# A hand-ordered RWKV and Hyena kernel with a new order of operations, banks, engine choices and POOL waits

## The chip, the cores and the metric

The kernel runs on one NeuronCore of a Trainium2 chip. The core has five engines, each with its own instruction queue that it works off strictly in order: PE (TensorE, matrix products, written to the eight banks of PSUM), DVE (VectorE), ACT (ScalarE), POOL (GpSimd) and SP (SyncE, which here only issues DMA transfers). The engines wait for one another through semaphores. The metric is the time of one execution on the device in microseconds (us).

## The reference

Two layers follow each other, in float32, for 4 batches of 768 steps with 8 heads of 48 (384 channels):

```python
for t in range(S):                                   # RWKV
    cur = np.einsum('bhd,bhe->bhde', u[None] * kt, vt)
    y[:, :, t] = np.einsum('bhd,bhde->bhe', rt, state + cur)
    state = wt[:, :, :, None] * state + np.einsum('bhd,bhe->bhde', kt, vt)
...
proj = x @ w_proj                                    # Hyena gate, x = y with heads side by side
x1, x2, x3 = proj[..., :D], proj[..., D:2*D], proj[..., 2*D:]
x2_conv = np.fft.irfft(np.fft.rfft(x2, axis=1) * np.fft.rfft(filter_fft, axis=0), n=S, axis=1)
return (x1 * x2_conv * x3) @ w_out
```

## The kernel before, in words

The 768 steps of a batch are cut into 6 chunks of 128, 24 chunks in all. `group` (line 1286) makes the operations that two neighbouring chunks share (the first two chunks go alone, so there are 13 groups: 0 is chunk 0, 1 is chunk 1, 2 is chunks 2 and 3, up to 12 for chunks 22 and 23). `first` (line 1321) makes those of one chunk. `early` (line 1495) and `spectrum` make the Fourier matrices and the spectrum of the filter, `second` (line 1593) the Hyena layer of one batch.

An operation has a name, and the string `ORDER` (line 45) has one line for each: the name, a letter for the engine, the PSUM bank if it opens one, and at the end, for POOL operations, the name of a DVE operation for which it is to wait although it needs nothing of it (a "tie"; the tie keeps POOL away from the SBUF port that it shares with DVE). `Plan.run` (line 1069) issues the operations in the order of this string, which is then each engine's program order; nothing else is scheduled. Letters: P, Q and F are PE (three ways of one product), A and N ACT, D, V and M DVE, G and C POOL, S SP, and a dash says that the operation is left out because its neighbour does its work. `warm n b` issues n/2 matmuls of 512 columns into bank b that nobody reads ("fillers", line 1225).

The names that matter below, i a chunk, g a group, b a batch:

- loads, on SP: `lw`, `lk`, `lr`, `lv` with i (192 KB each), `u`, three `lwproj`, `lwout`, `filt`
- head: `ur` and `um`, `ub` spread u over the partitions (copy, matmul, copy); `ang`, `sin`, `maps`, `masks`, `ia`, `is` make masks and Fourier matrices; `table` loads ACT's function table; `if` (line 1531) and `in` (line 1539) write signed copies of the inverse Fourier matrix, `in` with two products with -1.0, of 768 and of 192 elements a partition; `kz` clears padding
- RWKV: `ln`g logarithm of w, `cs`i its running sums on PE, `ex`i their exponentials, `kq`i products with k and r, `tr`i and `qk`i transposes and their copy, `sc`i scores, `mt`i masked scores (`mc`i is the mask when POOL makes it), `kv`i, `ki`i and `su`i the state, `rk`g = r times k, `ru`g times u, `rh`g adds the halves, `cc`g sums them, `vb`g is v in bf16, `vc`g is `vb` times `cc`; `yi`i, `ys`i, `y`i collect the output on PE, `xn`i copies it (with V it also adds `vc`, and `yi` is left out), `yt`i and `xT`i transpose it
- Hyena: `p`, `q` (with b, columns, half) and `xw` are the three projections, `cp`, `cq`, `cxw` their copies or products, `gq` the gate product if `cq` was only a copy, `sd`b.z.n sums and differences of the two halves of x2, `f` the forward transform, `cf` its copy, `u0`b, `u1`b and `p`b the product with the filter's spectrum (two products, one sum), `E` the inverse transform, `cE`, `aE`, `dE`, `yE` its copy, sums and gating, `o`, `co`, `so` the output product, its copy and its store; `h`, `hg`, `hc`, `fsd` are the filter's spectrum

An operation on two chunks works on tiles of 128 partitions by 768 elements. The buffers are few (line 41): three for w, four for k and r, four for v, and 8 PSUM banks for all products, so an order also sets when buffers come free.

Of the kernel before, what the change touches and what calls it, by code (L numbers as in the profile page):

```python
# [44 lines left out]
ORDER = """  # L45
table sin
wz D
pads D
lw3 S
u S  # L50
kz2 G
lw1 S
lw0 S
lk1 S
maps G
kz3 G
smalls D
lr0 S
lw2 S
lr1 S  # L60
lk0 S
ang2 D
lk2 S
lr2 S
lk3 S
lv0 S
ur A
warm 7 6
um P 7
ub A  # L70
sin2 A
ang1 D
sin1 A
kz1 G ang1
ang0 D
sin0 A
table exp
ln1 A
masks G ang0
imaps G ang0  # L80
ln0 A
lr3 S
lw5 S
lr4 S
lv1 S
lw4 S
ia2 G ang0
lv3 S
lv2 S
lk4 S  # L90
warm 32 5
cs1 P 6
lr5 S
lk5 S
cs0 P 1
ex1 A
kz0 D
kq1 D
warm 12 5
tr1 P 0  # L100
ex0 A
lwproj0 S
rk1 G
kq0 D
# [24 lines left out]
vb0 A
mt1.0 M  # L130
warm 7 2
tr2 P 5
lwproj1 S
qk2 A
lr7 S
mt1.1 -
sc0 P 2
sc2 P 4
mt2.0 M
mc2.0 -  # L140
mt2.1 -
mt0.1 -
mc0.1 -
mc1.1 -
lr6 S
lk7 S
lk6 S
table sin
is A
lv7 S  # L150
lw8 S
lv6 S
filt S
lw9 S
lr9 S
lk8 S
lk9 S
lr8 S
vb1 A
lv9 S  # L160
lv8 S
rh0 G
kv0 P 0
su0 D
mt0.0 M
mc0.0 -
warm 21 1
ki1 P 2
kv1 P
cc0 D  # L170
table exp
ln3 A
kq3 D
mc1.0 -
mc2.1 -
vb2 A
rk2 G
ph3 A
cc1 D
ru2 D  # L180
rh2 D
warm 4 5
tr3 P 3
# [12 lines left out]
kq4 D
vc2 G rh2
kv2 P
yi0 P 6
ph4 A  # L200
yt1 P 3
cs5 P 4
xT1 A
ex5 A
yi2 - 0
lw11 S
lw10 S
# [12 lines left out]
yt0 P 7  # L220
lk10 S
lr11 S
lr10 S
lwout S
rk3 G rh2
lk11 S
ru3 D
ki3 P 2
tr5 P 3
yt2 P 6  # L230
rh3 D
# [12 lines left out]
cc3 D
ys3 P
mt4.0 M
vb3 A
sc5 P 2
mt5.0 N
ln4 A  # L250
lw13 S
lw12 S
mt5.1 -
mc4.1 -
mt3.1 -
mc3.1 -
p0.0.0 P 0
y3 P
xn3 V
mc4.0 -  # L260
mc5.1 -
vc3 G rh3
lr12 S
lk13 S
lk12 S
cp0.0.0 A
ki4 P 4
kv4 P
# [12 lines left out]
yt3 P 2
xT4 A
y5 P
cp0.2.0 A
xT3 A
q0.0.0 P 6
xn5 V
if G
cq0.0.0 D
yt5 P 2  # L290
cs7 P 4
cs6 P 0
cwproj1 A
ex7 A
xw0.0 P 6
cxw0.0 A
xT5 D
xw0.2 P 2
xw0.4 P 6
kq7 D  # L300
rk4 G
ex6 A
ph7 A
cxw0.2 A
# [12 lines left out]
sd0.0.0 D
cc4 D
q0.0.1 P 4
sd0.1.0 D  # L320
sc7 P 2
qk6 A
sc6 P 0
mt6.1 -
cq0.0.1 D
mt6.0 M
mc6.0 -
gq0.0.1 -
vb4 A
f0.0 P 6  # L330
kv6 P 4
q0.2.1 P 5
mt7.0 N
su6 D
cq0.2.1 D
vc4 G sd0.1.0
cf0.0 A
mt7.1 -
mc7.1 -
mc6.1 -  # L340
mc7.0 C sd0.1.0
in A
yi6 P 2
y6 P
xn6 A
yi7 P 0
f0.2 P 6
ki7 P 4
ys7 P
kv7 P  # L350
ln5 A
lw15 S
# [48 lines left out]
u00.0 D
u10.0 D
p0.0 D
lw16 S
# [3 lines left out]
ru5 G fsd1  # L408
rh5 G
cxw1.0 A  # L410
sc9 P 4
q0.2.0 P 7
cc5 D
cq0.2.0 D
su9 D
gq0.2.1 -
lw17 S
lk16 S
mt8.1 -
# [12 lines left out]
kq11 D
cwout A
E0.0 P 4
E0.1 P 6
mc8.0 C p0.0
ph10 A
vc5 G p0.0
cE0.1 A
lr16 S  # L440
ph11 A
yi8 P 0
ys8 P
cE0.0 A
mc9.1 -
gq0.0.0 -
aE0.1.0 D
aE0.1.1 D
aE0.0.0 D
aE0.0.1 D  # L450
dE0.0.1 -
dE0.1.1 -
mc8.1 -
y8 P
E0.2 P 2
vb6 A
tr10 P 6
xn8 A
tr11 P 0
cE0.2 A  # L460
qk10 A
ki10 P 5
yt8 P 4
kv10 P
qk11 A
aE0.2.1 D
aE0.2.0 D
sc10 P 6
xT8 A
sc11 P 0  # L470
# [453 lines left out]
sd3.0.1 D
sd3.1.2 D
E2.1 Q 6
cq3.0.0 D
sd3.1.1 G sd3.1.2
co1.0 A
co1.1 A  # L930
# [8 lines left out]
aE2.1.1 D
aE2.1.0 D  # L940
sd3.0.0 G gq2.0.1
p3.2.0 P 0
# [3 lines left out]
aE2.2.1 D
aE2.2.0 D
cp3.2.0 A
dE2.2.0 D
# [96 lines left out]
"""

class Op:  # L1050
# [824 lines left out]
```

## Time and profile before

| what | us |
|---|---|
| runs | 156.36 (median), 155.32 and 156.45 |
| the profiled execution, its own time | 155.63 |
| its span, first to last instruction | 153.5 |

The profile's page names engines as above; PEld is PE's load of weights, which runs beside its products. Busy shares are over the span, and the lines with an L are lines of the kernel's file. In views in order of time each row begins with the start and the length in us, and a bracket at its end gives the idle time of the engine ahead of it and what ended it. In rows of groups, `x11 | 20.0, 1819 | 15.8` means 11 instructions, 20.0 us in all, 1819 ns for one, and 15.8 us of idle time just ahead of them. The most costly groups are spread thin: none of them is over 28 of the 153.5 us. DMA moves 27.40 MB in 104117 packets, of which 100129 are under 512 bytes.

### The profile page before, as it was taken

To read this page: it belongs to the slowest core of one execution; us is meant where nothing else is said; L and a number is where in the kernel's file an instruction comes from. 1 tells how busy PE (TensorE), PEld (TensorE's weight loads), DVE (VectorE), ACT (ScalarE), POOL (GpSimd) and SP (SyncE) were. 2 spreads that over 40 slices of the span, in tenths; PEclk is the share of its full clock that TensorE was granted. 3 is DMA by queue.
4 is the path that set the end of the run, shared out by engine and by line. 5 is a ranking of instruction groups with operands and counts; after the bars stand their busy time and mean duration, and the time that the engine had idled before them with its cause. 6 is when DMAs were issued, how large, how long until landed. Compare 5 with 4: busy or idle time off the path is not lost.

```text
span 153.5 us, 4271 instructions
## 1 busy us (share of the span) xinstructions
PE 141.5 (92%) x1666; PEld 89.0 (58%) x1666; DVE 127.9 (83%) x237; ACT 128.0 (83%) x225; POOL 76.9 (50%) x85
## 2 busy tenths in 40 slices
PE   4999888799999998999999999999999999999880
PEld 1345446556657564677666676686767665655530
DVE  6307894976599999999999699999999899999930
ACT  4868998897999999895999898998999557774570
POOL 7822949189541563997072913469461801410310
PEclk9999999999999999999999999999999999999999
DMA  4999979899899899999898999989940000700185
GB/s 86 218 207 221 218 150 268 157 345 204 184 315 208 155 192 279 195 212 211 159 207 163 225 193 207 216 168 204 275 161 4 0 4 0 307 0 4 70 323 223
DMA packets 104117, 27.40 MB, mean 178 GB/s; under 512 B 100129, under 2 KB 102690, under 8 KB 104098
## 3 DMA queue, kind: packets, MB, share of 16 engines
q1 hardware_dynamic: 104098, 27.14, 77.8%
q8 instruction: 13, 0.21, 0.6%
q14 instruction: 6, 0.05, 0.1%
HBM read 22.41 MB, written 4.72 MB: 177 GB/s over the span
## 4 chain that ended last, share of the span: by engine, by line
PE 53%; DVE 27%; ACT 8%; issue 4%; POOL 2%; DMA 1%; POOLq 1%; ACTq 0%; SPq 0%; DVEq 0%
PE banks L1600 11%; PE banks L1640 6%; DVE U L1189 6%; PE banks L1350 5%; PE banks L1490 4%; PE banks L1225 4%; PE banks L1362 4%; PE banks L1441 3%; PE banks L1776 3%; DVE kq L1338 3%; ACT banks L1335 3%; DVE mt L1378 2%; PE banks L1704 2%; PE banks L1461 2%; DVE P L1677 2%
## 5 line engine op out<-in xcount | busy, mean ns | idle before, releaser
L1189 POOL TENSOR_TENSOR rk<-kr 128x768 bf16<-128x768 f32 (+1 forms) x13 | 22.0, 1693 | 21.6 <-DMA kr<-in_r_dram 6.9
L1338 DVE TENSOR_TENSOR kq<-banks,kr 128x768 bf16<-128x768 f32 x24 | 22.5, 952 | 10.3 <-ACT banks L1335 10.2
L1600 PE MATMUL banks<-xT,wproj 128*128 128x384 bf16 x144 | 27.5, 326 | 0.0
L1189 POOL TENSOR_TENSOR vc<-vb,cc 128x768 bf16<-128x768 bf16 (+1 forms) x13 | 17.8, 1375 | 16.6 <-ACT vb L1193 6.8
L1193 ACT ACTIVATE x<-banks 128x768 bf16<-128x768 f32 (+1 forms) x29 | 20.1, 704 | 3.1 <-PE banks L1640 1.5
L1335 ACT ACTIVATE banks<-banks 128x768 f32<-128x768 f32 x24 | 19.0, 809 | 1.9 <-PE banks L1332 1.3
L1378 DVE TENSOR_TENSOR mt<-banks,mask_excl 128x1024 bf16<-128x1024 f32 (+1 forms) x17 | 18.9, 1124 | 0.8 <-PE banks L1362 0.7
L1600 PEld LDWEIGHTS <-wproj 128*128 128x128 bf16 x144 | 12.8, 97 | 7.3 <-issue 0.3
L1234 ACT ACTIVATE qk<-banks 128x512 f32<-128x512 f32 x24 | 14.0, 599 | 1.4 <-PE banks L1350 1.2
L1350 PE MATMUL banks<-ident,kq 128*128 128x128 bf16 x192 | 13.9, 219 | 0.8 <-ACT X L1193 0.3
L1225 PE MATMUL banks<-wt 128*128 128x512 bf16 (+1 forms) x43 | 13.3, 464 | 1.1 <-DVE wt L1256 1.1
L1776 PE MATMUL banks<-wout,y 128*128 128x384 bf16 x72 | 13.5, 326 | 0.6 <-DVE g L1626 0.5
L1490 PE MATMUL banks<-sd,F 128*128 128x384 bf16 (+1 forms) x96 | 13.7, 327 | 0.0
L1640 PE MATMUL banks<-wproj,xT 128*128 128x384 bf16 x72 | 13.4, 326 | 0.1
L1350 PEld LDWEIGHTS <-kq 128*128 128x128 bf16 x192 | 11.4, 97 | 3.4 <-DVE kq L1338 2.0
L1193 ACT ACTIVATE o<-banks 128x768 f32<-128x768 f32 (+1 forms) x13 | 9.6, 762 | 3.5 <-PE banks L1776 3.5
L1453 DVE TENSOR_TENSOR xn<-banks,vc 128x384 bf16<-128x384 f32 x17 | 9.2, 551 | 3.5 <-PE banks L1441 3.5
L1383 POOL TENSOR_SCALAR_AFFINE_SELECT mt<-mt 128x1024 bf16<-128x1024 bf16 (+1 forms) x10 | 9.5, 954 | 5.0 <-ACT banks L1335 4.0
L1193 ACT ACTIVATE X<-banks 128x768 bf16<-128x768 f32 x12 | 9.7, 809 | 2.8 <-PE banks L1490 2.8
L1189 DVE TENSOR_TENSOR U<-X,hh 128x2304 bf16<-128x2304 bf16 (+1 forms) x12 | 11.5, 995 | 0.0
L1490 PEld LDWEIGHTS <-F 128*128 128x128 bf16 (+1 forms) x120 | 8.3, 104 | 5.3 <-issue 0.9
L1704 PE MATMUL banks<-mi,P 128*128 128x384 bf16 (+1 forms) x62 | 10.4, 300 | 0.6 <-ACT banks L1335 0.6
(109 smaller groups left out, 309.1 us busy)
## 6 DMA issues: line engine op xcount, KB each, us to landing
w<-in_w_dram SPq DMA_DIRECT2D x24, 192.0 KB, 3.7
kr<-in_k_dram SPq DMA_DIRECT2D x24, 192.0 KB, 4.0
kr<-in_r_dram SPq DMA_DIRECT2D x24, 192.0 KB, 3.9
v<-in_v_dram SPq DMA_DIRECT2D x24, 192.0 KB, 4.1
out_dram<-o SPq DMA_DIRECT2D x11, 384.0 KB, 2.7
y<-in_moe_w_proj_dram SPq DMA_DIRECT2D x2, 576.0 KB, 5.5
U<-in_moe_filter_fft_dram SPq DMA_DIRECT2D x1, 1152.0 KB, 6.7
sd<-in_moe_w_proj_dram SPq DMA_DIRECT2D x1, 576.0 KB, 5.8
```

The costliest lines, as they stand in the source:

```text
L1189: return eng(e).tensor_mul(o, a, b)
L1193: return nc.scalar.activation(out=o, in_=a, func=AF.Copy)
L1225: nc.tensor.matmul(banks[:, int(at), 0:256 * z], wt[:, 0:L], _mid(wt, z), start=True, stop=True)
L1234: nc.scalar.activation(out=o.bitcast(FP32), in_=a.bitcast(FP32), func=AF.Copy)
L1335: op(f"ex{i}", [ACT], lambda e, bk: nc.scalar.activation(out=two(bk, f"cs{i}")[:, :, 0:C], in_=two(bk, f"cs{i}")[:, :, 0:C], func=AF.Exp), ...
L1338: op(f"kq{i}", [DVE], lambda e, bk: nc.vector.tensor_mul(kq[f][:, :, :, 0:D], two(bk, f"cs{i}")[:, :, 0:C].rearrange("p a (h d) -> p a h d ...
L1350: nc.tensor.transpose(p[:, HP * m + j, :], kq[f][:, m, 2 * j:2 * j + 2, :], ident)
L1378: return copy(ACT, o, x) if e in (ACT, ACT2) else nc.vector.tensor_mul(o, x, _mid(mask_excl, z - HP * a))
L1490: nc.tensor.matmul(p[rows], F[:, ti, c0 + rows.start:c0 + rows.stop], x[q][:, ti, :], start=(ti == 0), stop=(ti == NT - 1),)
L1600: nc.tensor.matmul(p, wproj[:, cb, col0:col0 + L], xT[bx][:, NT * hf:NT * hf + NT, cb, :], start=(cb == 0), stop=(cb == CB - 1),)
L1640: nc.tensor.matmul(view(bk)[:, z], xT[bx][:, c0 + z, cb, :], wproj[:, cb, C:2 * C], start=(cb == 0), stop=(cb == CB - 1),)
L1776: nc.tensor.matmul(view(bk)[:, z], yt_[:, z, :], wout[:, cb, :], start=(cb == 0), stop=(cb == CB - 1),)
```

## The change

Only the string `ORDER` is changed; no function is. The operations are the same 990, with the same dependences; what changes is the order on each engine's queue, the bank of 41 of them, the engine of 51, POOL's ties, and the fillers.

- Head: `u` and `ur` come first; `table sin` goes behind `ur`; the 32 fillers go ahead of everything else on PE, `um` behind `cs2`; the loads of r2 and v0 go ahead of k1, w2 and r1. `kz1` to `kz3`, `ia0`, `ia2`, `rk0`, `rh0`, `rh1`, `qk2` and the masked scores of chunks 0 and 2 go to DVE; `kz0`, `ia1` and `rh2` to POOL. Fillers grow from 83 to 101 (each counts for 256 columns).
- Before 45 us: `ru3`, `rh3` and `vb3` go to POOL (from DVE, DVE and ACT), `in` goes from ACT to POOL, where it stands behind `if` and ahead of `rk4`; `vc2` from POOL to DVE; `cp0.0.0`, `xT3`, `xT4` and `cxw0.2` from ACT to DVE. `sd0.0.0` stands ahead of `ru4` on DVE. `yi0` on PE is left out, `xn0` on DVE adds what it added.
- Middle: `rh5` to DVE; `rh7`, `ru9`, `rh10`, `rh11` and `ru12` to POOL; `xT12`, `xT16`, `xT18` and `xT20` from ACT to DVE; `cq0.2.1` and `cq2.2.1` to ACT as copies, for which `gq0.2.1` and `gq2.2.1` come up on DVE.
- Tail: `gq2.0.0` goes ahead of `xn23`, `dE1.2.0` behind it; `sd3.1.2` and `gq3.2.1` to POOL, `cq3.2.1` to ACT, `gq3.2.0` and `co3.2` to DVE; `yE3.1.0` on POOL loses its tie to `yE3.0.0`.
- Ties: most of POOL's ties name an earlier DVE operation than before, some are gone.

```diff
--- before.py
+++ after.py
@@ -42,1006 +42,1009 @@
...
-ORDER = """
+ORDER = """u S
+ur A
...
+kz2 D
...
+warm 32 5
...
+table exp
...
-kz2 G
...
-ur A
...
+cs1 P 0
...
-um P 7
...
+um P 6
...
+warm 2 7
...
+warm 12 1
...
+warm 2 3
...
+table sin
...
+warm 21 5
...
-warm 32 5
-cs1 P 6
...
-warm 12 5
...
-warm 7 2
...
-table sin
...
+warm 7 7
...
+warm 4 2
...
+vc2 D
...
+rk3 G cc0
...
+warm 2 3
...
+yi0 - 6
...
-warm 21 1
...
-table exp
...
-warm 4 5
...
-vc2 G rh2
...
-yi0 P 6
...
+ru3 G cc2
...
+rh3 G
...
-rk3 G rh2
...
-ru3 D
...
-rh3 D
...
+vb3 G xn2
...
+warm 12 4
...
-vb3 A
...
+if G su4
...
+in G
...
-if G
...
+rk4 G xn5
...
-rk4 G
...
+sd0.0.0 D
...
-sd0.0.0 D
...
+vc4 G kq6
...
-cq0.2.1 D
-vc4 G sd0.1.0
...
-in A
...
+cq0.2.1 A
...
+gq0.2.1 D
...
 kq9 D
...
+ru5 G su7
...
+rh5 D
...
+u00.0 D
...
-u00.0 D
...
-p0.0 D
...
-ru5 G fsd1
-rh5 G
...
+p0.0 D
+mc8.0 C u00.0
...
-gq0.2.1 -
...
-mc8.0 C p0.0
...
-yE0.1 D
...
-rk8 G yE0.2
...
+yE0.1 D
...
+rk8 G kq15
...
+u11.0 D
...
+ru10 G u11.0
...
+rh10 G cq1.2.1
...
-u11.0 D
...
-ru10 G p1.0
...
-rh10 D
...
+rh11 G aE1.0.1
...
-rh11 D
...
-ru12 D
...
+ru12 G
...
+dE1.2.1 D
...
+vc12 G yE1.0
...
-vc12 G yE1.0
...
-dE1.2.1 D
...
-gq2.2.1 -
+gq2.0.0 D
...
-dE1.2.0 D
...
-dE1.1.1 G dE1.2.0
...
+dE1.1.1 G mt23.0
...
+dE1.2.0 D
...
-gq2.0.0 D
...
+gq2.2.1 D
...
+sd3.0.2 D
...
 sd3.0.1 D
-sd3.1.2 D
...
+sd3.1.2 G sd3.0.2
...
-sd3.0.2 D
...
+cq3.2.1 A
...
-cq3.2.1 D
...
-gq3.2.1 -
...
+gq3.2.0 D
...
+gq3.2.1 G gq3.2.0
...
-gq3.2.0 G gq3.0.1
...
-yE3.1.0 G yE3.0.0
...
+yE3.1.0 G
...
-co3.2 A
...
+co3.2 D
...
```

More of the change, by code (lines that the diff above doesn't have):

```diff
@@ L134 @@
[L134 to L147, printed above, removed]
-table sin
-is A
-lv7 S
+ln1 A
+lr4 S
+lw5 S
+masks G ang0
+ln2 A
+imaps G kz3
+ia2 D
+lr3 S
+lv3 S
+cs1 P 0
+warm 7 6
+cs2 P 4
+ex1 A
+kq1 D
+um P 6
+vb0 A
+ln0 A
+ph1 A
+lv2 S
+lw4 S
+ub A
+warm 2 7
+tr1 P 0
+lv1 S
+ex2 A
+cs0 P 2
+rk1 G ang1
+ia0 D
+lr5 S
+lv5 S
+lk4 S
+ex0 A
+lk5 S
+kq2 D
+kq0 D
+warm 12 1
+qk1 A
+cs3 P 6
+ph0 A
+rk0 D
+ru1 D
+sc1 P 0
+lv4 S
+mt1.0 M
+mt1.1 -
+lwproj0 S
@@ L151 @@
+lw7 S
+lwproj2 S
+lw6 S
+ia1 G
+ex3 A
+ph2 A
+warm 2 3
+kv0 P 5
+lwproj1 S
+table sin
+lr6 S
+tr0 P 4
+tr2 P 3
+lk7 S
+su0 D
+warm 21 5
+lr7 S
+qk2 D
+kq3 D
+sc2 P 0
+qk0 A
+is A
+sc0 P 2
+lk6 S
+table exp
+ph3 A
+ru0 G
+mt2.1 A
+ln3 A
+vb1 A
+rk2 G mt1.0
+rh1 D
+rh0 D
+ru2 D
+cc1 D
+tr3 P 5
+warm 7 7
+mt0.1 D
+mt0.0 D
 lw8 S
 lv6 S
+mc1.0 -
+lv7 S
+mt2.0 D
+cc0 D
+vb2 A
+mc2.0 -
+warm 4 2
 filt S
 lw9 S
+qk3 A
+lk9 S
 lr9 S
+cs4 P 0
+ki1 P 2
+rh2 G ru2
+mc0.0 -
+mc2.1 G ru2
+ex4 A
+cc2 D
+vc2 D
@@ L243 @@
+kv3 P
+rh3 G
+yt0 P 3
+mc3.0 -
+mt3.1 -
+mc3.1 -
+cwproj0 A
 su3 D
 cc3 D
-ys3 P
+qk5 A
+qk4 A
+xT0 A
+lw11 S
+yi3 - 0
+yt2 P 6
+lr11 S
+ys3 P
+vb3 G xn2
+y3 P
+warm 12 4
+sc5 P 2
+sc4 P 4
+lk10 S
+xn3 V
+lwout S
+xT2 A
+lr10 S
 mt4.0 M
-vb3 A
-sc5 P 2
 mt5.0 N
-ln4 A
-lw13 S
-lw12 S
+mt4.1 -
+ki4 P 7
+yt3 P 6
+p0.0.0 P 0
+vc3 G mt3.0
 mt5.1 -
+cp0.0.0 D
+p0.2.0 P 5
 mc4.1 -
[L255 to L259, printed above, removed]
-mc4.0 -
[L261 to L268, printed above, removed]
@@ L439 @@
-cE0.1 A
-lr16 S
-ph11 A
 yi8 P 0
 ys8 P
+kq11 D
+gq0.0.0 -
+mc8.1 -
+lv14 S
+gq0.2.0 -
+cE0.1 A
+ph11 A
+rk6 G rh5
+y8 P
 cE0.0 A
-mc9.1 -
-gq0.0.0 -
 aE0.1.0 D
-aE0.1.1 D
[L449 to L458, printed above, removed]
+xn8 A
+aE0.0.1 D
+vb6 A
+E0.2 P 2
+tr10 P 1
+aE0.0.0 D
+aE0.1.1 D
+cE0.2 A
 tr11 P 0
-cE0.2 A
 qk10 A
+yt8 P 4
+qk11 A
+aE0.2.0 D
+lv15 S
+ru6 G aE0.0.0
+aE0.2.1 D
 ki10 P 5
-yt8 P 4
 kv10 P
-qk11 A
-aE0.2.1 D
-aE0.2.0 D
+lk17 S
 sc10 P 6
+su10 D
@@ L820 @@
 f2.1 P 0
-rh11 D
+sc20 P 6
+so0.0 S
 cc11 D
-vc11 G rh11
-sc20 P 6
 ph22 A
@@ L926 @@
[L926 to L930, printed above, removed]
+o1.2 P 0
 cE2.1 A
-o1.2 P 0
+E2.2 Q 2
+aE2.1.1 D
 co1.2 A
-E2.2 Q 2
+sd3.1.1 G p2.0
 cE2.2 A
-gq2.0.1 D
 E2.0 Q 4
+aE2.1.0 D
 cE2.0 A
[L939 to L942, printed above, removed]
+p3.2.0 P 1
+gq3.0.0 -
+aE2.2.0 D
+aE2.2.1 D
+sd3.1.2 G sd3.0.2
+dE2.1.0 D
+so1.0 S
 f3.2 P 6
+cp3.2.0 A
 f3.2.1 P
-sd3.0.2 D
[L946 to L949, printed above, removed]
 aE2.0.1 D
-dE2.2.1 G dE2.2.0
+aE2.0.0 D
 cf3.2 A
-aE2.0.0 D
+sd3.0.0 G
 dE2.0.0 D
-u03.2 D
```

1087 lines of the change are left out of this document (502 added, 585 removed).

## The prediction, made before the changed kernel was run

> **What bounds the kernel now.** I read the page's first part, then the engines' busy time in five stretches, then the chain of work that ended last, and then single stretches in order of time.
>
> ```profile
> span 153.5 us, 4271 instructions
> ...
> PE 141.5 (92%) x1666; PEld 89.0 (58%) x1666; DVE 127.9 (83%) x237; ACT 128.0 (83%) x225; POOL 76.9 (50%) x85
> ```
>
> The shares say little, because the limit changes. The stretches (start and end, length, busy time of PE, PEld, DVE, ACT and POOL, granted clock, DMA share, GB/s) show it:
>
> ```profile
> 0.00:10.20 10.20, 8.12 (x22) 2.73 (x23) 4.05 (x27) 6.99 (x9) 6.88 (x27) 1.00 0.84 167
> 10.20:36.90 26.70, 23.39 (x337) 14.92 (x335) 19.68 (x33) 23.98 (x42) 16.94 (x18) 1.00 1.01 223
> 36.90:67.40 30.50, 29.10 (x350) 18.36 (x351) 27.41 (x42) 29.26 (x52) 17.50 (x14) 1.00 1.00 218
> 67.40:122.60 55.20, 55.04 (x791) 38.05 (x790) 52.35 (x88) 49.34 (x93) 30.45 (x24) 1.00 0.82 173
> 122.60:153.50 30.90, 25.86 (x172) 14.97 (x169) 24.41 (x50) 18.43 (x32) 5.16 (x6) 0.99 0.30 116
> ```
>
> From 10 to 67 us the DMA engines are full (1.01 and 1.00). From 67 to 123 PE is busy 55.04 of 55.20 us: nothing but less matmul work shortens that. In the last stretch DVE is busy 24.41 us. So a gain can come from the head, from what DVE loses between about 40 and 60, or from the tail. The chain (start, length, what) says the same of both ends; the last line is DVE's own last run, to 147.39:
>
> ```profile
> 4.22 6.13 PE banks L1225 x16
> 10.79 0.80 ACT banks L1335
> ...
> 144.84 0.37 DVE y L1189
> ...
> 145.34 0.95 POOLq L1870
> ...
> 146.33 1.98 PE banks L1776 x11
> ...
> 146.22 1.17 DVE L1189 TENSOR_TENSOR y<-y,g 128x384 bf16<-128x384 bf16 x4
> ```
>
> It begins with 16 filler matmuls (line 1225) and, near the end, passes through one POOL product.
>
> **The change, part by part.** The sum is made against the profiled execution, 155.63 us, which lies 0.73 below the median of 156.36.
>
> *Head.* Now the fillers stand behind um, which waits for u, and cs1 stands behind the fillers:
>
> ```profile
> 8.53 0.94 ACT L1301 ACTIVATE lg<-w 128x384 bf16<-128x384 f32 x2
> 10.79 1.50 ACT L1335 ACTIVATE banks<-banks 128x768 f32<-128x768 f32 x2 [1.32 <-PE banks L1332]
> ...
> 37.66 0.96 DVE L1338 TENSOR_TENSOR kq<-banks,kr 128x768 bf16<-128x768 f32 x1 [0.54 <-ACT banks L1335]
> 39.65 0.96 DVE L1338 TENSOR_TENSOR kq<-banks,kr 128x768 bf16<-128x768 f32 x1 [1.03 <-ACT banks L1335]
> ...
> 31.05 4.17 SPq L1295 DMA_DIRECT2D kr<-in_k_dram x2
> ...
> DMA to landing us min/median/max: 3.6/6.3/6.7
> ```
>
> After the change the fillers come first and u's copy stands ahead of the sine table's load, so ln1 stays near 8.5 to 9.0, while cs1 no longer waits for fillers. ex1 then starts behind ln1 and ln2, near 9.9 instead of 10.79: 0.9 us early. In SP's queue u goes ahead of w3, and r2 and v0 ahead of k1: the load of r1, for kq1, is the eighth large one where it was the seventh, 192 KB at 167 GB/s or 1.2 us later, which can eat the lead at once. And it is not kept in any case. kq6 (39.65) needs the k load of chunk 6, the second of the pair that is issued from 31.05 to 35.2; with the shortest landing of 3.6 us after its issue it cannot be there before 38.8, and the queue ahead of it holds the same loads in both orders. So at most 0.85 us of lead survives at 40, and I keep 0.25. If the DMA cover were gone, the whole 0.9 would stay. Eighteen more fillers of 256 columns are queued (101 for 83); by the chain's 6.13 / 32 = 0.19 us each they cost at most 3.4 us, on a PE that idles 26.70 - 23.39 = 3.3 us in that stretch, and below nothing they cannot go. I take zero, since each stands where the next matmul waits for a copy, and leave their harm to the upper end.
>
> *POOL from rk3 to rk4.* ru3, rh3 and vb3 move to POOL, into one idle time; `in`, the two negations of line 1542, moves from ACT into another:
>
> ```profile
> 31.22 1.48 POOL L1189 TENSOR_TENSOR vc<-vb,cc 128x768 bf16<-128x768 bf16 x1 [3.62 <-ACT vb L1193]
> ...
> 39.51 1.82 POOL L1189 TENSOR_TENSOR rk<-kr 128x768 bf16<-128x768 f32 x1 [0.97 <-issue]
> ...
> L1189 POOL TENSOR_TENSOR rk<-rk,u_b 128x768 bf16<-128x768 bf16 x3 | 4.9, 1639 | 3.0 <-DVE P L1677 2.9
> L1311 POOL TENSOR_TENSOR rk<-rk 128x384 bf16<-128x384 bf16 x2 | 1.8, 910 | 0.2
> L1195 POOL CAST vb<-v 128x768 bf16<-128x768 f32 x1 | 0.8, 822 | 2.7 <-DVE sd L1651 2.7
> L1536 POOL TENSOR_SCALAR mi<-mi 128x384 bf16<-128x384 bf16 x1 | 1.2, 1167 | 0.0
> ...
> 41.36 0.56 DVE L1189 TENSOR_TENSOR rk<-rk,u_b 128x768 bf16<-128x768 bf16 x1 [0.75 <-POOL rk L1189]
> ```
>
> The three cost 1.64 + 0.91 + 0.82 = 3.37 us and fit into 3.62. `in` writes 768 + 192 = 960 elements a partition. No row shows it on POOL. Low end, at the cast's 822/768 ns an element: 1.0 us. High end, at L1536's 1167/384: 2.9 us. L1536 is the nearest, also a product with -1.0 on the same tile, so I take 2.9. Of it 0.97 is idle time; vc2's move to DVE lets rk3 and all behind it start earlier by up to a product's 1.48; I take 0.6, an estimate, since rk3 waits for loads too. rk4 so comes 2.9 - 0.97 - 0.6 = 1.3 later, and ru4 on DVE starts as rk4 ends, as it does now at 41.36. Against that, the new order puts sd0.0.0 (0.75) ahead of ru4, into the wait. Net 0.3 to 0.7 us later on DVE at 45; I take 0.5 (with the low end it would be 0.6 early). Behind rk4 on POOL stands vc4, and y6 on PE waits for vc4 through yi6; PE has room there, as f0.0 and q0.2.1 stand in between. The Trainium skill, page "GPSIMD Engine Reference", section "Engine selection", calls one-input operations on GpSimd roughly line-rate; by that `in` would cost about the low end and the sum would be 1.1 us better; the L1536 row differs.
>
> *DVE from 45 to 63.* cq0.2.1 leaves DVE (0.55); its later product gq0.2.1 and rh5 come to it (0.355 each): +0.16. Two losses go. kq9 waits 0.37 for its exponential, which stood behind `in` on ACT. And U's first product meets POOL's rh5:
>
> ```profile
> 50.01 0.96 DVE L1338 TENSOR_TENSOR kq<-banks,kr 128x768 bf16<-128x768 f32 x1 [0.37 <-ACT banks L1335]
> ...
> L1189 DVE TENSOR_TENSOR U<-X,hh x2: 1343/1610/1876, 55.5 to 57.3; 128x2304 bf16<-128x2304 bf16 x2
> ...
> 55.26 0.91 POOL L1311 TENSOR_TENSOR rk<-rk 128x384 bf16<-128x384 bf16 x1
> ...
> L1626 DVE TENSOR_TENSOR g<-banks,x 128x384 bf16<-128x384 f32 x7 | 3.9, 550 | 0.0
> L1311 DVE TENSOR_TENSOR rk<-rk 128x384 bf16<-128x384 bf16 x9 | 3.2, 355 | 0.2
> L1189 DVE TENSOR_TENSOR y<-y,g 128x384 bf16<-128x384 bf16 x5 | 1.5, 355 | 0.1
> ```
>
> The same product took 1.876 and 1.343 us: the first, from 55.50, ended 1.2 us after rh5 did, so it stood until POOL was done. With rh5 on DVE 0.53 us are saved. Together 0.16 - 0.37 - 0.53 = -0.74, and with +0.5 from above -0.25 at 63. If the loads held DVE back again, this would be zero.
>
> *From 63 to 123.* The same matmuls run (yi0, two of them, goes), on a full PE; some 16 operations change engine or waits. New waits of DVE are those of cc10, cc11, cc12 and rh9 on halves and products that POOL now makes (0.91 and 1.64, above); behind each waits DVE's whole queue, but other work stands between, and POOL is busy only 30.45 of these 55.20 us. I take 0, with -0.5 to +1.0 for small waits.
>
> *Tail.* After xn23, DVE loses gq2.0.0 (now ahead of it), sd3.1.2 (to POOL) and cq3.2.1 (to ACT), and gains dE1.2.0, gq2.2.1 and gq3.2.0:
>
> ```profile
> L1189 DVE TENSOR_TENSOR g<-g,x 128x768 bf16<-128x768 bf16 x3 | 1.8, 598 | 0.0
> L1651 DVE TENSOR_TENSOR sd<-x 128x384 bf16<-128x384 bf16 x4 | 1.3, 368 | 0.0
> L1747 DVE TENSOR_TENSOR y<-y 128x384 bf16<-128x384 bf16 x7 | 2.4, 358 | 0.1
> ...
> 130.47 0.69 DVE L1189 TENSOR_TENSOR g<-g,x 128x768 bf16<-128x768 bf16 x1
> ...
> 145.36 0.91 POOL L1189 TENSOR_TENSOR y<-y,g 128x384 bf16<-128x384 bf16 x1 [1.43 <-DVE y L1189]
> ```
>
> That is 0.60 + 0.37 + 0.55 = 1.52 out and 0.36 + 0.355 + 0.355 = 1.07 in: -0.45. The stretched gq2.0.1 (0.69) may lose 0.1. yE3.1.0 on POOL no longer waits for yE3.0.0: it ends near 145.3 instead of 146.27. Next late is the last product of block 2, inside DVE's run of four from 146.22, so only some 0.25 of that 1.0 reaches the end. co3.2 on DVE beside co3.3 on ACT gives at most 0.1, since its store follows co3.3's on SP. Tail: -0.8, from -0.3 to -1.2.
>
> Sum: -0.25 - 0.8 = -1.05. The profiled execution would be 154.6, the median 156.36 - 1.05 = 155.3.
>
> **Rivals.**
>
> *More.* `in` at its low end (-1.1) and the head's 0.65 kept: 155.3 - 1.75 = 153.6. For it: ACT is relieved of several copies where it was busy 23.98 of 26.70. Against it: the DMA share of 1.01.
>
> *Nothing moves.* The loads hold everything up to 67, and in the tail another wait takes POOL's place: 155.3 + 0.25 + 0.5 = 156.05. For it: DMA and PE are full in turn, for 112 of 153 us.
>
> *Slower: POOL takes the port first.* Many POOL operations are now tied to the operation before a DVE product with two SBUF tiles, not to that product: mc8.0 ahead of p0.0, ru10 ahead of p1.0, rk8 ahead of yE0.1, vc12 ahead of dE1.2.1, dE1.1.1 ahead of gq2.0.0, sd3.1.2 ahead of sd3.0.1. All is well if DVE asks first.
>
> ```profile
> 97.69 1.35 DVE L1189 TENSOR_TENSOR U<-X,hh 128x2304 bf16<-128x2304 bf16 x1
> 99.08 1.36 DVE L1677 TENSOR_TENSOR P<-U 128x2304 bf16<-128x2304 bf16 x1
> ...
> 100.58 1.64 POOL L1189 TENSOR_TENSOR rk<-rk,u_b 128x768 bf16<-128x768 bf16 x1 [2.89 <-DVE P L1677]
> ```
>
> DVE's next product began 0.04 us after the one that it needs (97.69 + 1.35 = 99.04, then 99.08); a released POOL operation began 0.14 after (99.08 + 1.36 = 100.44, then 100.58). The margin is 0.1 us, for DVE. Where it fails, DVE loses the POOL operation's length, 0.9 to 1.8 us; it decides as soon as one longer than the gain of 1.05 is lost. One at 1.3 gives 156.6, three give 155.3 + 3.9 = 159.2. The Trainium skill, page "Perfetto Trace Analysis", section "Optimizing Scalar/DVE Operations", warns that moving work between DVE and GpSimd might not help, because they share a port; here ru10's 1.64 us lie beside unstretched DVE work.
>
> **How the numbers follow.** About 1% (1.56 us, so 154.8 and 157.9) is what a measurement of this kernel can tell from no change. Forecast, 154.3 to 156.0: 0.47. More, 153.0 to 154.3: 0.22. Nothing, 156.0 to 156.6: 0.17. Slower, above 156.6: 0.14. Faster by over 1% is the second case and a quarter of the first, 0.34; slower by over 1% is most of the last, 0.12; the rest is 0.54. The range leaves out the lower half of the second case and two thirds of the last, 0.2: 153.6 to 157.2.
>
> **What would show it.** Right: cs1 near 9.0; the two POOL negations of `in` at about 2.9 us together, rk4 near 41; U's products both 1.35; PE still full from 67 to 123; POOL's yE3.1.0 ending before DVE's yE3.0.0 does. Wrong: any DVE product with two SBUF inputs stretched by more than 0.5 us, PE gaps between 67 and 123 adding to over 1 us, or kq6 starting before 38.8.

## The result and the profile after

| | before | after |
|---|---|---|
| median of 20 runs each, us | 156.22 (155.16 to 158.38) | 157.06 (156.28 to 158.05) |
| the profiled execution, its own time, us | 155.63 | 156.87 |
| its span, us | 153.5 | 155.2 |

The ratio of after to before is 1.0062, with a 95% interval from 1.0038 to 1.0087. The changed kernel is 0.6 to 1.4 us slower, where 1.05 us less was forecast. Every ratio here and below leaves out runs more than 1.5% above the fastest of their kernel and is taken against runs of the kernel before made beside them on the same chip; medians are of all runs. First the head of the page after, then its five stretches (start and end, length, busy time of PE, PEld, DVE, ACT and POOL, granted clock, DMA share, GB/s):

```profile
span 155.2 us, 4297 instructions
...
PE 142.7 (92%) x1673; PEld 90.5 (58%) x1673; DVE 132.4 (85%) x250; ACT 125.4 (81%) x216; POOL 90.3 (58%) x88
```

```profile
0.00:10.20 10.20, 8.38 (x33) 3.45 (x33) 4.36 (x31) 9.34 (x12) 4.45 (x22) 1.00 0.81 162
10.20:36.90 26.70, 23.61 (x328) 14.92 (x328) 22.24 (x39) 20.52 (x36) 19.22 (x18) 1.00 1.03 232
36.90:67.40 30.50, 27.47 (x292) 16.89 (x291) 27.06 (x40) 25.14 (x44) 19.11 (x13) 0.94 0.95 208
67.40:122.60 55.20, 55.19 (x806) 38.49 (x804) 52.23 (x87) 50.70 (x95) 39.16 (x29) 1.00 0.82 168
122.60:155.20 32.60, 28.04 (x222) 16.73 (x220) 26.53 (x55) 19.69 (x33) 8.32 (x9) 0.98 0.31 122
```

The third row is the odd one. Before, PE issued 350 matmuls there; now it issues 292, and the granted clock is 0.94 where it was 1.00. To see where the time went, the rows of both timelines were matched operation by operation, by their order on each engine:

| operation | before | after | later by |
|---|---|---|---|
| kq6 ends (DVE) | 40.61 | 41.10 | 0.49 |
| rk4 ends (POOL) | 41.33 | 44.27 | 2.95 |
| cq0.0.1 ends (DVE) | 44.97 | 47.38 | 2.41 |
| h1 starts (PE) | 49.44 | 53.15 | 3.71 |
| p0.0 ends (DVE) | 60.04 | 63.26 | 3.22 |
| yi8 starts (PE) | 62.76 | 65.70 | 2.94 |
| y23 starts (PE) | 122.26 | 124.63 | 2.37 |
| co3.2 ends (last copy) | 149.91 | 151.38 | 1.47 |

So 3.7 us are lost between 38 and 53 us, and 2.2 of them come back later. The loss starts on POOL. This is POOL's timeline of the changed kernel (start, length, in brackets the idle time ahead and what ended it):

```profile
39.17 3.32 POOL L1547 TENSOR_SCALAR mn<-mi 128x768 bf16<-128x768 bf16 x2
42.46 1.82 POOL L1192 TENSOR_TENSOR rk<-kr 128x768 bf16<-128x768 f32 x1
...
49.54 2.24 POOL L1192 TENSOR_TENSOR rk<-kr 128x768 bf16<-128x768 f32 x1 [0.65 <-DMA kr<-in_k_dram]
```

The first row is `in`, the second rk4 behind it, the third rk5, which a load releases. DVE's timeline shows both effects:

```profile
41.18 0.76 DVE L1654 TENSOR_TENSOR sd<-x 128x1152 bf16<-128x1152 bf16 x1
44.31 0.56 DVE L1192 TENSOR_TENSOR rk<-rk,u_b 128x768 bf16<-128x768 bf16 x1 [2.37 <-POOL rk L1192]
...
46.43 0.95 DVE L1629 TENSOR_TENSOR g<-banks,x 128x768 bf16<-128x768 f32 x1
...
48.70 4.29 DVE L1556 TENSOR_TENSOR P<-U 128x1152 bf16<-128x1152 f32 x2
```

DVE idles 2.37 us for rk4 (0.75 before). The last row is fsd0 and fsd1 with 4.29 us for the two, where the same two took 46.75 to 49.37, 2.62, before: fsd1 alone took 2.96 instead of 1.35, because it overlaps rk5 from 49.54 to 51.77. The row `g<-banks,x` is cq0.0.1, which empties PSUM bank 4. Before, the kernel had these rows for cq0.0.1, fsd0 with fsd1, kv6 and f0.2:

```profile
44.02 0.95 DVE L1626 TENSOR_TENSOR g<-banks,x 128x768 bf16<-128x768 f32 x1
...
46.75 2.62 DVE L1553 TENSOR_TENSOR P<-U 128x1152 bf16<-128x1152 f32 x2
...
45.03 0.31 PE L1403 MATMUL banks<-vb,kq 128*64 128x48 bf16 x8
...
46.54 1.14 PE L1490 MATMUL banks<-sd,F 128*128 128x384 bf16 x6
```

On PE of the changed kernel, kv6 needs bank 4:

```profile
44.20 1.15 PE L1493 MATMUL banks<-sd,F 128*128 128x384 bf16 x6
47.44 0.31 PE L1406 MATMUL banks<-vb,kq 128*64 128x48 bf16 x8 [2.09 <-DVE g L1629]
...
48.95 2.09 PE L1493 MATMUL banks<-sd,F 128*128 128x384 bf16 x6
```

PE idles 2.09 us ahead of kv6. Behind the gap, the six matmuls of f0.2, of the same form as those in the first row (f0.0), take 2.09 us instead of 1.15. The same stretch in windows of 1 us shows the clock:

```profile
45.00:46.00 1.00, 0.35 (x3) 0.00 (x0) 0.96 (x3) 0.80 (x2) 0.00 (x0) 1.00 0.88 171
46.00:47.00 1.00, 0.00 (x0) 0.00 (x0) 1.00 (x2) 0.20 (x1) 0.65 (x1) 1.00 1.15 231
47.00:48.00 1.00, 0.56 (x10) 0.41 (x11) 1.00 (x2) 0.00 (x0) 1.00 (x2) 1.00 1.03 204
48.00:49.00 1.00, 1.00 (x14) 0.68 (x12) 1.00 (x3) 0.48 (x1) 0.89 (x1) 0.53 1.11 216
49.00:50.00 1.00, 1.00 (x8) 0.48 (x5) 1.00 (x1) 0.85 (x3) 0.46 (x1) 0.50 1.09 213
50.00:51.00 1.00, 1.00 (x6) 0.48 (x5) 1.00 (x2) 0.39 (x1) 1.00 (x1) 0.50 1.12 227
51.00:52.00 1.00, 1.00 (x20) 0.70 (x18) 1.00 (x1) 0.92 (x2) 0.77 (x1) 0.76 1.10 214
```

From 48 us on the granted clock (the third number from the end) is half, up to some 51.5. There are thus two delays side by side between 47 and 53: PE's (gap and half clock) and DVE's (fsd1). h1 stands behind kv7 on PE, which starts at 53.00, and all of h1 but its first matmul waits for fsd1, which ends at 52.99 (that the first one does not wait shows in the run with sd0.0.0 moved back, below). Where the experiments' expectations give 1.95 and 3.11 us for f0.2, these are the sums of its six matmuls' own times, which overlap.

### The profile page after: what moved, and what is told of

It is laid out like the page before. It is cut to its first block, busy times and chain, and to the rows that moved or that the text cites. A ratio compares the mean times of both kernels' runs of the same rounds, so it can differ in the third digit from the quotient of the medians.

```text
span 155.2 us, 4297 instructions
## 1 busy us (share of the span) xinstructions
PE 142.7 (92%) x1673; PEld 90.5 (58%) x1673; DVE 132.4 (85%) x250; ACT 125.4 (81%) x216; POOL 90.3 (58%) x88
## 4 chain that ended last, share of the span: by engine, by line
PE 74%; SPq 6%; DVE 6%; ACT 4%; DMA 3%; issue 2%; POOL 2%; DVEq 0%; POOLq 0%
PE banks L1603 14%; PE banks L1493 11%; PE banks L1779 8%; PE banks L1643 7%; SPq L1298 6%; PE banks L1353 6%; PE banks L1707 5%; PE banks L1444 4%; PE banks L1365 4%; PE banks L1464 3%; PE banks L1406 3%; DMA kr<-in_k_dram 3%; PE banks L1435 2%; PE banks L1332 2%; DVE U L1192 2%
## 5 line engine op out<-in xcount | busy, mean ns | idle before, releaser
L1196 ACT ACTIVATE x<-banks 128x768 bf16<-128x768 f32 (+1 forms) x27 | 18.6, 697 | 3.3 <-PE banks L1603 1.7
L1192 POOL TENSOR_TENSOR vc<-vb,cc 128x768 bf16<-128x768 bf16 (+1 forms) x12 | 17.1, 1426 | 5.7 <-ACT vb L1196 2.5
L1381 DVE TENSOR_TENSOR mt<-banks,mask_excl 128x1024 bf16<-128x1024 f32 (+1 forms) x18 | 18.4, 1040 | 1.1 <-PE banks L1365 1.0
L1386 POOL TENSOR_SCALAR_AFFINE_SELECT mt<-mt 128x1024 bf16<-128x1024 bf16 (+1 forms) x11 | 11.3, 1026 | 10.7 <-DVE U L1192 6.5
L1228 PE MATMUL banks<-wt 128*128 128x512 bf16 (+1 forms) x52 | 15.5, 441 | 2.1 <-DVE scl L1252 1.1
L1192 POOL TENSOR_TENSOR rk<-rk,u_b 128x768 bf16<-128x768 bf16 (+1 forms) x7 | 11.9, 1694 | 6.9 <-DVE rk L1192 3.1
L1493 PE MATMUL banks<-sd,F 128*128 128x384 bf16 (+1 forms) x96 | 14.7, 339 | 0.0
L1237 ACT ACTIVATE qk<-banks 128x512 f32<-128x512 f32 x23 | 13.4, 601 | 1.2 <-PE banks L1353 1.2
```

The costliest lines, as they stand in the source:

```text
L1192: return eng(e).tensor_mul(o, a, b)
L1196: return nc.scalar.activation(out=o, in_=a, func=AF.Copy)
L1228: nc.tensor.matmul(banks[:, int(at), 0:256 * z], wt[:, 0:L], _mid(wt, z), start=True, stop=True)
L1381: return copy(ACT, o, x) if e in (ACT, ACT2) else nc.vector.tensor_mul(o, x, _mid(mask_excl, z - HP * a))
L1493: nc.tensor.matmul(p[rows], F[:, ti, c0 + rows.start:c0 + rows.stop], x[q][:, ti, :], start=(ti == 0), stop=(ti == NT - 1),)
```

## The experiments

The theory: the whole loss comes from one line, `in` on POOL ahead of rk4; the collision on fsd1 and the half clock only follow from it. The rivals: the collision is a loss of its own (rk5's new tie), or the new order as a whole is worse, its head for instance.

### `in` moved out of the way

```diff
-in G
...
 ru5 G su7
+in G
```

> The changed kernel with one line moved: `in` stays on POOL, but stands behind ru5, in POOL's idle stretch from 55.5 to 62.0 us, not ahead of rk4. Theory (the whole loss hangs on `in` ahead of rk4): rk4 starts near 39.2 instead of 42.46, ru4 on DVE near 42.0 instead of 44.3, cq0.0.1 ends near 45.0; PE's idle time of 2.09 us ahead of kv6 goes, f0.2 takes 1.95 us instead of 3.11, and fsd1 is over (near 49.0) before the load lets rk5 start (near 49.5), so fsd1 takes 1.35. Time 2.5 to 3.3 us below the changed kernel: about 154.2 us, ratio to the kernel before 0.987. Rival (the port collision of rk5 with fsd1 is a loss of its own): fsd1 still over 2.5 us and the gain at most 1.5 us, 155.6. Rival (the order as a whole): within 0.5 us of the changed kernel, 156.6 to 157.1.

Measured: median 154.33 us, ratio to before 0.9842 (0.9756 to 0.9927); span 151.2. rk4 starts at 38.83, ru4 at 41.64 without a wait, cq0.0.1 ends at 44.71. PE's timeline of this kernel shows neither the gap nor the slow matmuls:

```profile
45.06 0.31 PE L1406 MATMUL banks<-vb,kq 128*64 128x48 bf16 x8
45.31 0.66 PE L1603 MATMUL banks<-xT,wproj 128*128 128x384 bf16 x3
...
46.17 1.14 PE L1493 MATMUL banks<-sd,F 128*128 128x384 bf16 x6
```

fsd1 takes 1.35 and is over at 49.13; rk5 starts at 49.62. One moved line turns the loss into a gain of 1.6%, by three runs with a wide interval; the last table has more. The theory holds. Not all is well here: fsd0 takes 1.84 us instead of 1.35, since mc7.0 still runs on POOL until 46.65. `in` itself now takes 5.37 us, of which more below.

### The collision and the clock, one without the other

The first kernel restores rk5's tie (it keeps `in` ahead of rk4); the second adds fillers to it, into PE's gap:

```diff
-rk5 G mt6.0
...
 fsd1 D
+rk5 G fsd1
```

```diff
 mt7.0 N
+warm 18 2
```

> The changed kernel with rk5 tied to fsd1 and listed behind it, as in the kernel before, and nothing else. Both theories: fsd1 takes 1.35 us instead of 2.96. Theory (PE has its own delay of the same size, from its idle time ahead of kv6 and slow matmuls behind it, and h1 starts when both are over): h1 still starts near 53.1 and the time falls by 0 to 0.4 us, to about 156.8, ratio 1.004. Rival (the collision is the loss): DVE and all behind it come 1.6 us earlier, about 155.5 us, ratio 0.995.

> As the run before, and besides 9 filler matmuls of 512 columns (1.9 us) on PE between f0.0 and kv6, where it idles 2.09 us. They compute nothing that is read. Theory (PE's idle time lowers its granted clock, and the clock is the second of two parallel delays): f0.2 takes 1.95 us instead of 3.11, h1 starts 0.9 to 1.2 us earlier, near 52.1, and the time falls by 0.9 to 1.2 us against the changed kernel, to about 156.0, although neither edit moves it alone. Rival (the clock falls there for another reason): f0.2 stays near 3.1 and h1 near 53.1, time as in the run before.

Measured: the tie alone 156.69 us, ratio 1.0009 (0.9963 to 1.0055), span 155.1; tie and fillers 155.69 us, ratio 0.9966 (0.9937 to 0.9996), span 154.1. In the profile of the tie alone fsd1 is back at 1.35 and h1 still starts at 53.08; DVE now waits for PE instead:

```profile
48.63 2.68 DVE L1556 TENSOR_TENSOR P<-U 128x1152 bf16<-128x1152 f32 x2
51.23 0.34 DVE L1192 TENSOR_TENSOR g<-g,x 128x384 bf16<-128x384 bf16 x1
53.28 0.36 DVE L1416 TENSOR_TENSOR S<-banks,phi 128x192 bf16<-128x192 f32 x1 [1.71 <-PE banks L1406]
```

With fillers in the gap the clock stays whole and f0.2 takes 1.14 from first to last; h1 starts at 52.04, 1.1 earlier:

```profile
48.00:49.00 1.00, 0.93 (x12) 0.51 (x12) 1.00 (x3) 0.34 (x1) 1.00 (x2) 1.00 1.02 197
49.00:50.00 1.00, 1.00 (x14) 0.65 (x12) 1.00 (x2) 0.89 (x3) 0.17 (x1) 1.00 1.05 209
```

So in this stretch the half clock follows from PE's idle time, and it is one of two parallel delays. The single runs agree. Of the nine runs of the tie alone that enter its ratio, four had a mean granted clock of 0.995 or more, with a median of 155.44 us, and five had 0.983 to 0.988, with a median of 156.86; with the gap filled, none of ten was below 0.992. Of the changed kernel's 20 runs, 9 had a clock of 1.0 (median 156.78) and 11 had 0.983 to 0.993 (median 157.37): there, with fsd1 late as well, the clock seems worth only 0.6 us. A mean clock does not say where the clock fell, though; only the profiled runs show that. The expectation spoke of the tie as worth 0 to 0.4 us. The interval of its ratio holds the 1.004 expected and not the rival's 0.995; by the single runs, 0 to 0.4 us is right where the clock falls, and too little where it does not.

### `in` alone on POOL, in the kernel before

```diff
 if G
...
+in G
 rk4 G
...
-in A
```

> The kernel before with one part of the change alone: `in` goes from ACT to POOL, ahead of rk4. Theory: rk4 starts 3.36 - 0.97 = 2.4 us later, near 41.9, ru4 2.4 later, near 43.8, PE idles about 2 us before it gets a bank of q0.0.1's back and its clock falls, and the time rises by 1.5 to 3 us, to 157.7 to 159.2, ratio 1.010 to 1.019. ACT's hour of 1.1 us for `in` that comes free gives at most 0.4 of it back (kq9's wait). Rival (the order as a whole): within 0.5 us of the kernel before.

Measured: 156.91 us, ratio 1.0101 (1.0041 to 1.0160); span 154.6 against 153.5. One line is enough to make the kernel before slower by about as much as the whole change did. rk4 starts at 41.27 and ru4 at 43.12, 1.76 late. But PE idled only 0.86 us ahead of kv6, and its clock stayed at 1.00 there, so the expectation was too high in that point, and 156.91 us lies below the 157.7 to 159.2 expected. fsd1 took 1.35. So DVE's delay alone, without the half clock at kv6 and without the collision, is enough for a loss: h1 starts 1.76 late and p0.0 ends 1.09 late. (Taking the line out of the changed kernel gave 2.2%, from 1.0062 to 0.9842; the difference fits the collision and the clock, which are added there.) This execution's clock did fall at another place, which the last section takes up. `in` is also shorter here. The tile `mn` (least, median and longest of the two instructions, ns) in this kernel and in the changed one:

```profile
L1543 POOL TENSOR_SCALAR mn<-mi x2: 687/1408/2128, 38.5 to 40.6; 128x768 bf16<-128x768 bf16 x1, 128x192 bf16<-128x192 bf16 x1
```

```profile
L1547 POOL TENSOR_SCALAR mn<-mi x2: 1228/1678/2128, 39.2 to 41.3; 128x768 bf16<-128x768 bf16 x1, 128x192 bf16<-128x192 bf16 x1
```

The long instruction takes 2128 ns in both; the short one 687 or 1228. In the changed kernel sd0.0.0, a DVE sum of two SBUF tiles, runs from 41.18 to 41.94 beside the short one; in the kernel before it stands behind ru4.

### sd0.0.0 moved back

```diff
-sd0.0.0 D
...
 ru4 D
...
 rh4 D
+sd0.0.0 D
```

> The changed kernel with DVE's sd0.0.0 moved back behind rh4, out of the wait for rk4. Theory (sd0.0.0, a product of two SBUF tiles, ran while `in` ran on POOL, and `in` stood meanwhile: its second instruction took 1.23 us against 0.69 undisturbed): `in` takes 2.8 us, rk4 starts 0.5 us earlier, near 41.9, and ru4 near 43.75; DVE then pays sd0.0.0's 0.75 behind it, so cq0.0.1 ends within 0.3 us of the changed kernel's 47.38, and the time is the changed kernel's within 0.4 us, ratio 1.003 to 1.009. Rival (`in` is slow for a reason of its own): `in` stays at 3.3 us and the time rises by 0.3 to 0.8.

Measured: 156.82 us, ratio 1.0046 (0.9996 to 1.0097); span 154.9. `in` takes 687 and 2127 ns, rk4 starts at 41.71 and ru4 at 43.56, cq0.0.1 ends at 47.17 instead of 47.38. The 0.54 us by which `in` was longer are the time in which POOL stood for sd0.0.0. In the run with `in` behind ru5 the same is seen larger: U's two products of 1.33 us and the sum rh5 between them ran beside the short instruction, and it took 3236 ns.

The Trainium skill says on the page "SBUF — State Buffer", sections "SBUF: two separate sides" and "Who interferes with whom", that DVE and GpSimd share one pair of SBUF ports, that a DVE instruction with two SBUF inputs contends for it with a GpSimd one that reads SBUF, and that whichever starts first holds it for its whole instruction. The times above agree (1228 and 3236 ns for 687), and so does fsd1's behind rk5 (2.96 us for 1.35); the run with `in` between mc7.0 and rk5, below, agrees in the sharing and not in the whole instruction (0.62 us of wait for 2.13 us of `in`).

The same run also mends PE's delay without DVE's. PE's gap ahead of kv6 is 0.86 us here, the clock stays at 1.00 and f0.2 takes 1.14; but fsd1 still takes 2.96 us beside rk5, and ends at 52.78. PE reaches h1 early and then stands for fsd1:

```profile
51.54 0.33 PE L1493 MATMUL banks<-P,F 128*64 128x384 bf16 x1
52.84 2.22 PE L1493 MATMUL banks<-P,F 128*64 128x384 bf16 x17 [0.96 <-DVE P L1556]
```

p0.0 ends at 62.87, only 0.39 earlier than in the changed kernel. So mending either of the two delays alone gives little: the tie mends DVE's, this run PE's, and the kernel with tie and fillers both.

### The tail alone and the head alone

The first kernel has the order of before up to y23 and the changed order behind it; the second has the changed order up to q0.0.0, ahead of `in`, and the order of before behind it.

> The kernel before up to y23 (122.3 us), and the changed kernel's order from there. Theory (the prediction's tail, -0.8): gq2.0.1 and yE3.1.0 no longer stretch or wait, o3.2 ends near 148.0 instead of 148.78, span 152.6 to 152.9 instead of 153.5, ratio 0.995. Rival (the tail's gain depends on the order ahead of it): within 0.2 us of the kernel before.

> The changed kernel's order up to the matmuls of q0.0.0 (near 35 us), ahead of `in`, and the kernel before's order from there. This part moves ru3, rh3 and vb3 to POOL, the copies to DVE, the fillers, the loads and the sine table. Theory: the loads and PE hold kq6 near 39.6 whatever the head does, and the time is within 0.3 us of the kernel before, ratio 0.998 to 1.002; what the changed kernel lost is all behind this part. Rival (the head is a part of the loss): kq6 0.5 us later, as in the changed kernel, ratio 1.003 or more.

Measured, tail: 154.92 us, ratio 0.9941 (0.9903 to 0.9978). From y23's start to co3.2's end it took 122.78 to 149.34, 26.56 us, where the kernel before took 122.26 to 149.91, 27.65: 1.09 less. The span, 153.1, is above what was expected only because y23 started 0.52 later in this execution. The chain of waits shows why it is shorter; this is its end (start, length, what):

```profile
142.14 0.97 PE banks L1775 x6
143.11 0.65 PE banks L1703 x4
143.76 4.94 PE banks L1775 x30
```

Before, the chain's end went from DVE through POOL's yE3.1.0 to PE; now PE is never without work there, and POOL's product (143.71 to 144.62) is off the chain.

Measured, head: 155.77 us, ratio 1.0022 (0.9991 to 1.0054). kq6 starts at 40.06, which is 0.4 later than before and nearer to the rival; but cq0.0.1 ends at 44.91 (44.97 before), so nothing of it remains at 45. The interval holds no change and a loss of 0.5% alike. The head gives nothing; whether it costs a few tenths stays open.

### Where `in` can stand

Three more places were tried: on POOL between mc7.0 and rk5, where POOL waits for rk5's load; on POOL behind ru5 with rk5's tie restored; and on DVE ahead of ru4, with the same tie.

> The changed kernel with `in` on POOL between mc7.0 and rk5, where POOL waits 2.96 us for rk5's load once rk4 is early. Theory: DVE's fsd0 and fsd1 run back to back there; `in` (two instructions, 2.8 us undisturbed) is put off by them or puts them off once. If fsd0 and fsd1 stay at 1.35 us, rk5 starts 0.5 to 2.5 us later than 49.62, which nothing waits for, and the time is that of the run with `in` behind ru5, 153.5 to 154.5. Rival (GpSimd takes the port first): one of the two fsd products is stretched by 1 us or more and the time rises by 0.5 to 1 us against that run.

> The changed kernel with both: `in` behind ru5 on POOL, and rk5 tied to fsd1. Theory (the collision of rk5 with fsd1 came only from DVE being 2.4 us late, since the load holds rk5 until 49.6 and fsd1 is over at 49.1): the tie changes nothing, the time is that of `in` behind ru5 alone, near 154.3, ratio 0.984 to 0.988. Rival (the two losses add): 1 us or more below the run with `in` moved alone, 153.0 or less.

> As the run with `in` late and rk5 tied, but `in` on DVE, between sd0.0.0 and ru4, where DVE no longer waits. Theory: DVE pays its length there, by the nearest rows 0.3 to 0.7 us for 960 elements, all behind it to 60 us comes so much later, and the time is 0.2 to 0.7 us above that run: ratio 0.988 to 0.991. Rival (relieving POOL of 2.8 us gains more than DVE pays): ratio 0.985 or less.

| kernel | median us | ratio to before | span |
|---|---|---|---|
| between mc7.0 and rk5 | 153.63 | 0.9899 (0.9866 to 0.9933) | 151.9 |
| behind ru5, tie restored | 153.27 | 0.9857 (0.9821 to 0.9893) | 151.4 |
| on DVE ahead of ru4, tie restored | 154.18 | 0.9849 (0.9739 to 0.9959) | 153.0 |

In the first, fsd1 is stretched to 1.97 us: `in` got the port once ahead of it. That is the rival's mechanism at 0.62 us instead of 1, and the sum p0.0 ends 0.47 later than in the second kernel; the two ratios' intervals overlap. The long instruction of `in`, 2.13 us undisturbed, ran until 49.91, beside fsd1 (47.84 to 49.81): it held fsd1 up for 0.62 us, not for its whole length. The tie changes nothing once `in` is out of the way: the second kernel's ratio is that of the first experiment. It is the fastest version found with a narrow interval, 1.1 to 1.8% below the kernel before. On DVE, `in` is short:

```profile
L1547 DVE TENSOR_SCALAR mn<-mi x2: 204/279/354, 43.4 to 43.6; 128x768 bf16<-128x768 bf16 x1, 128x192 bf16<-128x192 bf16 x1
```

The 0.56 us lie within what was expected, but four scattered runs (153.04 to 155.08) cannot tell this place from the one behind ru5.

## Why the prediction was wrong, step by step

- **POOL from rk3 to rk4: the step that failed.** The prediction took `in` at 2.9 us, covered 0.97 of it with idle time and 0.6 with an earlier start, and had rk4 1.3 us later and DVE 0.5 later at 45. rk4 came 2.95 later and cq0.0.1 2.41. The length was right for `in` undisturbed (2.81). The earlier start was an unmeasured guess, and it came out with the other sign: `if` ended at 39.08, after 38.54 before. rk3 started only 0.10 earlier, since it waits for a load, and mc5.0, now tied to mt4.0 on DVE, waited 0.65 us for it ahead of `if`. These are POOL's rows of the changed kernel for rk3, mc5.0 and the last of `if`, and behind them the last of `if` before:

```profile
25.68 1.82 POOL L1192 TENSOR_TENSOR rk<-kr 128x768 bf16<-128x768 f32 x1 [0.33 <-DMA kr<-in_k_dram]
...
33.19 1.09 POOL L1386 TENSOR_SCALAR_AFFINE_SELECT mt<-mt 128x1024 bf16<-128x1024 bf16 x1 [0.65 <-DVE mt L1381]
...
37.91 1.17 POOL L1539 TENSOR_SCALAR mi<-mi 128x384 bf16<-128x384 bf16 x1
...
37.38 1.17 POOL L1536 TENSOR_SCALAR mi<-mi 128x384 bf16<-128x384 bf16 x1
```

  And sd0.0.0, which the prediction counted as put "into the wait", held `in` for 0.54 us there. Start 0.6 + 0.54 = 1.14 and length 3.36 - 2.9 = 0.46 make 1.60 of the 1.65 us (2.95 - 1.3) that were missed.
- **Who waits behind it.** The prediction named vc4, yi6 and y6 and held that PE had room. It did not follow ru4 to cq0.0.1, which empties the bank that kv6 needs. That made the gap of 2.09 us and, in the profiled run, the half clock behind it. No term of the sum stood for either.
- **The port.** The rival said that POOL might take the port ahead of DVE at the loosened ties, and gave DVE the better odds by 0.1 us. At the places it named this was right: DVE's operations kept their lengths, and POOL's were stretched instead.

```profile
62.00 2.21 POOL L1386 TENSOR_SCALAR_AFFINE_SELECT mt<-mt 128x1024 bf16<-128x1024 bf16 x1 [6.51 <-DVE U L1192]
...
102.08 2.75 POOL L1192 TENSOR_TENSOR rk<-rk,u_b 128x768 bf16<-128x768 bf16 x1 [1.51 <-DVE U L1192]
```

  These are mc8.0 (1.09 undisturbed) and ru10 (1.64). The one DVE operation stretched by 1.6 us was at a tie that the prediction did not list, rk5's. There a load released POOL, not a DVE operation, so the margin of 0.1 us meant nothing; POOL was released whenever the load landed, here in the middle of fsd0, and so stood first in line when fsd0 ended. The rival's size (one operation, 1.3 us, 156.6) fits what came, and the mark set for it, one stretched by over 0.5 us, was met by fsd1. That its time fits is luck: with the collision mended alone the ratio is still 1.0009, and with `in` moved alone the collision does not occur.
- **DVE from 45 to 63.** U's products both took 1.34, as forecast, and kq9's wait is gone. From h1 to p0.0 the delay falls from 3.71 to 3.22. The mechanism held, at about 0.5 of the 0.74 us.
- **63 to 123.** Forecast 0; between yi8 and y23 the delay falls from 2.94 to 2.37. The same 877 matmuls, to the end of y23, took 59.29 us instead of 59.85, in small pieces on a PE that its busy share (55.04 of 55.20) showed as full. What gave it is not shown.
- **Tail.** Forecast -0.8; 2.37 falls to 1.47, -0.90, and alone it measured -1.09. The steps were right: yE3.1.0 ended at 146.47, and yE3.0.0 started at 146.38 and ended at 146.73.
- **Head.** cs1 started at 8.40, where 9.0 was expected, and ex1 at 9.00, 1.8 us earlier than before where 0.9 was expected; a load took the lead at once, as described: kq1 waits 4.53 us for r1. Of the lead 0.25 was to remain; 0.49 of a delay did.

```profile
10.96 0.96 DVE L1341 TENSOR_TENSOR kq<-banks,kr 128x768 bf16<-128x768 f32 x1 [4.53 <-DMA kr<-in_r_dram]
```

- **The sum and the chances.** The 0.25 kept of the head's lead does not stand in the sum: the -0.25 there is DVE's, 0.5 less 0.74. With it the forecast would have been -1.3, further off. And the chances do not fit each other: 0.12 for times above 157.9 is more than the 0.09 left above 157.2.

The rule of the Trainium skill, page "GPSIMD Engine Reference", section "Engine selection", that one-input operations run roughly at line rate, was set against the row of line 1536 in the prediction. The row was right: 2.81 us for 960 elements a partition, against the low end of 1.0.

## What to carry to other kernels

When work is moved to an engine "with room", follow what is queued behind it there through every engine, down to the PSUM bank that the next matmul wants: `in` cost little on ACT or behind ru5, and 1 to 2% (1.0101 against 1, 1.0062 against 0.9857) where one product stood behind it. A sum made of ends of ranges should not count on an earlier start that no row shows. And where two delays run side by side, mending one shows little; mend both, or take away what causes them.

## What the runs showed of the hardware

- A gap of 2.09 us on PE, in a stretch of 3 us (45 to 48) with 0.91 us of matmul work, was followed by a granted clock of 0.50 to 0.53 for some 3.4 us (0.94 + 1 + 1 + 0.48, by twice the lack in each window); with the gap filled the clock stayed whole. The longest gap does not decide it alone. In the run with `in` alone on POOL a gap of 0.86 us at kv6 left the clock at 1.00, while in the same execution 3 us (21 to 24) with 2.10 us of matmul work and no gap over 0.65 us came ahead of another slow stretch:

```profile
24.00:25.00 1.00, 0.85 (x11) 0.50 (x8) 0.78 (x2) 0.74 (x4) 1.00 (x1) 0.87 0.90 223
25.00:26.00 1.00, 1.00 (x22) 0.76 (x21) 0.00 (x0) 0.59 (x2) 1.00 (x2) 0.50 1.04 362
```

  It lasted until some 28 us, again about 3.4 us by the same sum. The Trainium skill, page "TensorE: Matmul & The Clock Gate", section "What's actually happening", describes a free-running window of about 3.4 us after whose idle the clock is halved; the length of the slow stretches and the spread between runs agree, though PE was never idle for that long here. How little work in a stretch lowers the clock is not shown.
- POOL's product with a constant, of one SBUF input, stands still while DVE works on two SBUF tiles: 687, 1228 and 3236 ns for the same instruction beside none, beside one sum, and beside two products with a sum between them. The other way round, POOL's rk5 (1.82 us, two SBUF inputs) held fsd1 up for 1.6 us, and `in`'s long instruction (2.13 us, one SBUF input) only for 0.62.
- The same negation of 768 elements took 2128 ns on POOL, 836 on ACT and 354 on DVE.
